# Prologue of an adaLN + MQA + SwiGLU kernel: X tiles first, large weight loads held back, more tile places, evacuation on two engines, new scheduler estimates

## Chip, cores and metric

One core of one Trainium2 chip. Times are device microseconds (us) of that core. A comparison uses runs of the two kernels taken in the same rounds on one chip. The experiments ran on three chips, so kernels of different sessions are compared through their ratios to the kernel before, whose medians in the sessions (1311.0 to 1311.7 us) are close enough for totals to be set side by side to about 1 us. The kernel before takes 1310.71 us (median of 3 runs, 1310.08 to 1313.36).

## The reference, cut to what matters

```python
x: (1, 2048, 1024) bf16;  H = 32 query heads of 32, one key/value head;  F = 3584
mod = silu(c) @ w_mod                     # six vectors of 1024: sa, ca, ga, sb, cb, gb
h = layernorm(x) * (1 + ca) + sa
x = x + ga * attention(h; wq, wk, wv, wo) # softmax over all 2048 keys, no mask
h = layernorm(x) * (1 + cb) + sb
x = x + gb * ((silu(h @ w1) * (h @ w3)) @ w2)
```

Keys and values of all 2048 rows are needed before the first block of queries can be finished. That makes the prologue (load X, normalise, transpose, project to K and V) a gate for the attention.

## The kernel before

The kernel describes all work as a graph of nodes. A list scheduler then fixes, at build time, the order of instructions on every engine. It uses an estimate of each node's duration. The program fixes each engine's order, so **an estimate does not change how long an instruction takes; it changes what stands before it.**

```python
# estimates
def act_t(n):                 return n / 1200.0 + 0.115      # ScalarE: 0.968 us for 1024 elements
def dve_t(n, rate=1):         return n / rate / 960.0 + 0.08
MM = 512 / 2400.0 + 0.0026                                   # one 512-column matmul: 0.2159 us
# in schedule(): a DMA
st = max(dma_free, s + 1.2); dma_free = st + n.nbytes / 230e3
# in schedule(): TensorE takes scores ("S") as soon as they can start, then PV and
# denominators ("V", "D"), and fills what is left with other matmuls
def key(c):
    s, n = c
    if n.cls == "S":            r = 0
    elif n.cls is not None:     r = 1 if att or t - n.est > 1.0 else 4
    else:                       r = 3
    return (r, n.prio, n.seq)
```

The prologue (cut):

```python
xload(0, 4)                                        # X tiles 0-3, 256 KB each
for k in range(NC): dma(... WM01[:, k, :] ...)     # 8 x 512 KB: shift and scale weights
dma(... WKV ...); dma(... WQ[:, :, 0:P] ...)       # wk, wv, first piece of wq
xload(4, 4)
dma(... WQ[:, :, P:D] ...)                         # 1792 KB
dma(... WO ...)                                    # 2048 KB
# [...]
for tb in range(NTB):                              # four blocks of 512 rows
    for i in range(4): ln_stats(tb * 4 + i)        # VectorE
    ln_scale(tb * 4, 4)                            # GpSimd
    for i in range(4): ln_norm(tb * 4 + i, i)      # VectorE, into XN[0..3]
    if tb + 2 < NTB: xload(tb * 4 + 8, 4)          # X has 8 places
    ln_transpose(..., ("act", "dve") if tb == 0 else ("dve",))   # TensorE, evacuated by ScalarE / VectorE
    kv(tb)
    if tb == 0: qproj(0, 0)
```

The attention of one block of 512 queries has 8 groups of 4 heads and 16 tiles of keys, so 128 score steps. One step is four score matmuls (side by side in the array), two exponentials of 128x1024 on ScalarE, and some time later the product with V (PV). In all there are 512 score steps and 1024 exponentials. The kernel uses eight PSUM banks; the scores take six of them and everything else shares two. While ScalarE works on a step, TensorE runs "fillers": Q projections, then the output projection and the MLP (W1, W3, W2) of the block before. The last block's MLP has no attention left to hide behind.

The softmax here doesn't subtract the row's maximum and nothing guards it: scores larger than these inputs give would overflow.

## Time and profile before

Three parts of the page: share of busy time, and the slices of the span (one digit is a fortieth, in tenths).

```profile
span 1308.6 us, 21172 instructions
...
PE 1138.8 (87%) x8561; PEld 439.4 (34%) x8689; DVE 958.9 (73%) x1206; ACT 1015.3 (78%) x1142; POOL 17.1 (1%) x35
...
PE   5387896455779999999899999999999999999998
...
ACT  1368988999999999999979999998999998011100
...
PEclk8688996666889999999999999999999999999999
...
L656 ACT ACTIVATE UREG<-SP 128x1024 bf16<-128x1024 f32 x1024 | 968.5, 1067 | 85.5 <-PE SP L646 65.9
```

ScalarE is at 9 tenths for most of the span and at 0 or 1 in the last six slices, where TensorE is at 9 (8 in the last). So there are two regimes: ScalarE sets the pace until its last exponential, TensorE after it. The Trainium skill (Perfetto Trace Analysis, "Optimization Strategy") says that kernels can have regimes with different most-contended engines, and that interleaving them can pay; this trace has two such regimes.

The stretches of the next view are: to the 16th exponential, to 129, to the end of the Q projections, scores almost without fillers, attention with the MLPs, tail. Columns: stretch, length, then busy time and number of instructions of PE, PEld, DVE, ACT, POOL, then the granted TensorE clock, DMA share, GB/s.

```profile
0.00:49.50 49.50, 23.71 (x315) 14.58 (x321) 29.58 (x60) 19.36 (x22) 5.93 (x17) 0.84 0.84 290
49.50:129.00 79.50, 55.12 (x571) 24.53 (x571) 62.42 (x98) 47.52 (x51) 2.94 (x6) 0.78 0.32 100
129.00:213.00 84.00, 76.30 (x642) 27.74 (x648) 68.31 (x80) 78.10 (x84) 0.00 (x0) 0.95 0.09 26
213.00:373.00 160.00, 91.27 (x756) 24.34 (x763) 108.81 (x119) 146.86 (x158) 1.01 (x2) 0.68 0.09 19
373.00:1107.70 734.70, 698.59 (x5318) 258.03 (x5395) 613.07 (x729) 706.75 (x800) 5.76 (x8) 1.00 0.35 90
1107.70:1308.60 200.90, 193.85 (x980) 90.15 (x997) 76.71 (x122) 16.74 (x29) 1.47 (x3) 0.99 0.53 127
```

The last exponential ends at 1107.7 us; after it come 200.9 us of almost unbroken TensorE work. In the stretch 213 to 373 TensorE has no fillers until 335 us (then some of WO), and its clock was granted at 0.68. The Trainium skill (TensorE: Matmul & The Clock Gate, "What's actually happening") says that an idle array runs at half rate; a mean of 0.68 in the stretch with the most idle time of TensorE (68.7 of 160 us) agrees with the direction. The share of idle time alone does not give the clock, though: in the first stretch TensorE is idle for 52% of the time, and the clock was 0.84.

The timeline of ScalarE from 26 to 90 us shows the prologue's cost. Columns: start, length, engine, line, operation; in brackets the idle time before it and what ended it.

```profile
29.18 1.94 ACT L656 ACTIVATE UREG<-SP 128x1024 bf16<-128x1024 f32 x2 [8.00 <-PE SP L646]
35.36 3.77 ACT L656 ACTIVATE UREG<-SP 128x1024 bf16<-128x1024 f32 x4 [4.25 <-PE SP L646]
39.96 9.27 ACT L656 ACTIVATE UREG<-SP 128x1024 bf16<-128x1024 f32 x10 [0.82 <-PE SP L646]
73.86 7.44 ACT L656 ACTIVATE UREG<-SP 128x1024 bf16<-128x1024 f32 x8 [24.64 <-PE SP L646]
```

Sixteen exponentials run (keys of rows 0 to 1023), then nothing for 24.64 us. The timeline of the DMA queue (SPq) from 10 to 80 us says why:

```profile
17.00 2.89 SPq L409 DMA_DIRECT2D X<-in_A_x_dram  x4
19.94 0.43 SPq L422 DMA_DIRECT2D WREG<-in_A_wq_dram  x1
20.41 0.88 SPq L424 DMA_DIRECT2D WO<-in_A_wo_dram  x1
21.33 10.25 SPq L581 DMA_DIRECT2D WREG<-in_w_mod_dram  x3
31.70 39.35 SPq L409 DMA_DIRECT2D X<-in_A_x_dram  x16
```

And the timeline of VectorE from 44 to 62 us:

```profile
49.33 1.23 DVE L702 TENSOR_TENSOR UREG<-UREG 128x2048 bf16<-128x2048 bf16 x1 [0.60 <-ACT UREG L656]
50.47 1.28 DVE L461 BATCH_NORM_STATS2 ST<-X 128x6 f32<-128x512 bf16 x2
53.03 0.69 DVE L682 COPY ASB<-PB 128x512 f32<-128x512 f32 x1 [1.27 <-PE PB L670]
```

X tiles 8 to 15 are issued from 31.70 us on, behind wq (L422), wo (L424) and three modulation weights (L581); the last eight of the x16 are later loads, from 60.57 us. VectorE starts their statistics (L461) at 50.47 us. In its fixed order they stand behind the sums of the exponentials (L702), for which it waited 0.60 us just before. The queue is not the only cause: the first of these tiles had landed at 40.99 us, so the last 9.5 us before its statistics are due to VectorE's order, fixed beforehand by the scheduler.

To compare whole runs, I use the **delay** of ScalarE. A packed exponential is counted as 0.9246 us (12.94 us for 14 of them), an interleaved tanh as about 0.48 us. Delay at the n-th exponential = its start − (n − 1) × 0.9246 − 0.48 × tanh so far. Before: 29.2 us at the first, 59.1 at the 17th, 67.4 at the 69th, 74.9 at the 151st, 120.5 at the last.

The Trainium skill (ScalarE: Activation LUTs, "What ACT_TABLE_LOAD costs") gives 186 ns + 0.833 ns per element for an activation with immediate scale and bias and an overlap of about 93 ns; for 1024 elements that is 1039 − 93 = 946 ns, an estimate from the page; the trace has 904 from start to start.

### The profile page before, as it was taken

To read this page: it belongs to the slowest core of one execution; us is meant where nothing else is said; L and a number is where in the kernel's file an instruction comes from. 1 tells how busy PE (TensorE), PEld (TensorE's weight loads), DVE (VectorE), ACT (ScalarE), POOL (GpSimd) and SP (SyncE) were. 2 spreads that over 40 slices of the span, in tenths; PEclk is the share of its full clock that TensorE was granted. 3 is DMA by queue.
4 is the path that set the end of the run, shared out by engine and by line. 5 is a ranking of instruction groups with operands and counts; after the bars stand their busy time and mean duration, and the time that the engine had idled before them with its cause. 6 is when DMAs were issued, how large, how long until landed. Compare 5 with 4: busy or idle time off the path is not lost.

```text
span 1308.6 us, 21172 instructions
## 1 busy us (share of the span) xinstructions
PE 1138.8 (87%) x8561; PEld 439.4 (34%) x8689; DVE 958.9 (73%) x1206; ACT 1015.3 (78%) x1142; POOL 17.1 (1%) x35
## 2 busy tenths in 40 slices
PE   5387896455779999999899999999999999999998
PEld 3133331111223333333333333333333333444443
DVE  5768786666798888778978887789888887643421
ACT  1368988999999999999979999998999998011100
POOL 1000000000000000000000000000000000000000
PEclk8688996666889999999999999999999999999999
DMA  9415104000003333342423333441533334375545
GB/s 313 151 41 178 33 1 110 12 1 1 1 1 97 98 97 97 94 85 57 120 78 94 95 94 94 93 77 29 157 97 98 97 97 85 77 175 147 160 83 118
DMA packets 253504, 118.93 MB, mean 91 GB/s; under 512 B 121312, under 2 KB 245216, under 8 KB 253408
## 3 DMA queue, kind: packets, MB, share of 16 engines
q1 hardware_dynamic: 253408, 117.59, 33.9%
q8 instruction: 68, 1.11, 0.4%
q14 instruction: 28, 0.23, 0.1%
HBM read 113.38 MB, written 4.19 MB: 90 GB/s over the span
## 4 chain that ended last, share of the span: by engine, by line
PE 58%; ACT 25%; DVE 9%; issue 6%; DMA 1%; POOL 1%; SPq 0%; DVEq 0%; ACTq 0%
ACT UREG L656 24%; PE PB L765 13%; PE PB L794 10%; PE PB L670 8%; PE SP L646 7%; PE SP L765 6%; PE SP L794 4%; PE PB L546 3%; PE PB L738 2%; ACT HREG L774 2%; DVE UREG L697 2%; DVE ST L461 1%; DVE UREG L702 1%; PE PB L712 1%; PE SP L738 1%
## 5 line engine op out<-in xcount | busy, mean ns | idle before, releaser
L656 ACT ACTIVATE UREG<-SP 128x1024 bf16<-128x1024 f32 x1024 | 968.5, 1067 | 85.5 <-PE SP L646 65.9
L765 PE MATMUL PB<-QT,WREG 128*128 128x512 bf16 x1397 | 343.3, 381 | 9.1 <-issue 6.4
L702 DVE TENSOR_TENSOR UREG<-UREG 128x2048 bf16<-128x2048 bf16 x256 | 310.5, 1213 | 38.4 <-ACT UREG L656 35.9
L646 PE MATMUL SP<-QT,KT 32*128 32x512 bf16 x2048 | 215.4, 411 | 100.0 <-ACT UREG L656 93.9
L697 DVE TENSOR_TENSOR UREG<-UREG 128x2048 bf16<-128x2048 bf16 x128 | 155.8, 1217 | 70.0 <-ACT UREG L656 69.9
L765 PEld LDWEIGHTS PB<-QT,WREG 128*128 128x128 bf16 x1456 | 125.7, 98 | 176.2 <-issue 52.3
L646 PEld LDWEIGHTS SP<-QT,KT 32*128 32x128 bf16 x2048 | 52.0, 92 | 313.4 <-ACT UREG L656 287.0
L794 PE MATMUL PB<-HREG,WREG 128*128 128x512 bf16 x612 | 153.3, 380 | 4.0 <-issue 2.5
L670 PE MATMUL PB<-UREG,V 128*32 128x512 bf16 x2016 | 142.9, 419 | 6.2 <-ACT UREG L656 5.8
L721 DVE RECIPROCAL DSB<-DSB 128x128 f32<-128x128 f32 x128 | 115.5, 928 | 0.1
L774 ACT ACTIVATE HREG<-SP 128x512 bf16<-128x512 f32 x28 | 16.7, 597 | 126.8 <-PE SP L765 123.9
L781 DVE TENSOR_TENSOR HREG<-HREG,PB 128x512 bf16<-128x512 bf16 x98 | 66.3, 676 | 19.6 <-PE PB L765 18.6
L794 PEld LDWEIGHTS PB<-HREG,WREG 128*128 128x128 bf16 x644 | 55.3, 98 | 73.5 <-issue 22.9
L765 PE MATMUL SP<-QT,WREG 128*128 128x512 bf16 x330 | 74.5, 379 | 0.3
L670 PEld LDWEIGHTS PB<-UREG,V 128*32 128x32 bf16 x2016 | 48.0, 101 | 78.9 <-issue 32.4
L776 DVE SCALAR_TENSOR_TENSOR HREG<-HREG,PB 128x512 bf16<-128x512 bf16 x84 | 57.5, 685 | 13.0 <-ACT HREG L774 9.9
L546 PE MATMUL PB<-HREG,WREG 128*128 128x512 bf16 x243 | 62.2, 389 | 1.7 <-DVE QT L549 0.8
L774 ACT ACTIVATE HREG<-PB 128x512 bf16<-128x512 f32 x84 | 56.5, 672 | 6.9 <-PE PB L765 6.8
L794 PE MATMUL SP<-HREG,WREG 128*128 128x512 bf16 x245 | 56.0, 379 | 0.4
L738 PE MATMUL PB<-WO,QT 128*128 128x512 bf16 x193 | 51.0, 389 | 2.9 <-DVE X L741 1.2
L776 DVE SCALAR_TENSOR_TENSOR HREG<-HREG,SP 128x512 bf16<-128x512 bf16 x28 | 19.3, 688 | 43.4 <-ACT HREG L774 43.4
L765 PEld LDWEIGHTS SP<-QT,WREG 128*128 128x128 bf16 x336 | 32.8, 98 | 39.4
(81 smaller groups left out, 547.9 us busy)
## 6 DMA issues: line engine op xcount, KB each, us to landing
WREG<-in_B_w_dram SPq DMA_DIRECT2D x112, 512.0 KB, 3.9
WREG<-in_B_w_dram SPq DMA_DIRECT2D x32, 896.0 KB, 5.9
X<-in_A_x_dram SPq DMA_DIRECT2D x32, 256.0 KB, 3.6
WREG<-in_w_mod_dram SPq DMA_DIRECT2D x16, 512.0 KB, 5.0
UREG<-in_w_mod_dram SPq DMA_DIRECT2D x8, 512.0 KB, 7.9
out_dram<-X SPq DMA_DIRECT2D x16, 256.0 KB, 2.6
WO<-in_A_wo_dram SPq DMA_DIRECT2D x1, 2048.0 KB, 14.6
WREG<-in_A_wq_dram SPq DMA_DIRECT2D x1, 1792.0 KB, 9.6
```

The source lines that it names most:

```text
L546: g = mm_group(NC, lambda e, b, c: e.matmul(b, WQ[:, c, f * P:(f + 1) * P], HT[:, c, sl], start=c == 0, stop=c == NC - 1), lambda c: [("WQ ...
L646: r = e.matmul(SP[:, bufs[gg // 2], gg % 2, j * qn:(j + 1) * qn], KT[32 * gg:32 * gg + 32, kt * P:(kt + 1) * P], QT[32 * gg:32 * gg + 32, ...
L656: G.add("act", lambda e, u=u, h=h, b=bufs[h]: e.activation(U[:, u, 2 * h:2 * h + 2, 0:npk * qn], SP[:, b, :, 0:npk * qn], ACT.Exp, scale=S ...
L670: r = e.matmul(PB[g.bank][32 * gg:32 * gg + 32, 0:qn], V[:, kt, :], U[:, pu, gg, j * qn:(j + 1) * qn], start=w0 + n == 0 and j == 0, stop= ...
L697: G.add("dve", lambda e, tr=tr, u=u, fu=first_u: e.tensor_tensor(TR[:, tr, :, 0:npk * qn], U[:, fu, :, 0:npk * qn], U[:, u, :, 0:npk * qn] ...
L702: G.add("dve", lambda e, tr=tr, u=u: e.tensor_tensor(TR[:, tr, :, 0:npk * qn], TR[:, tr, :, 0:npk * qn], U[:, u, :, 0:npk * qn], ALU.add), ...
L721: G.add("dve", lambda e, h=h: e.reciprocal(DSB[:, h * 128:(h + 1) * 128], DSB[:, h * 128:(h + 1) * 128]), reads=["DSB"], writes=[("DSBr", ...
L738: g = mm_group(NC, lambda e, b, f, t=t, h=h: e.matmul(b, QT[:, f, t * P:(t + 1) * P], WO[:, f, h * 512:(h + 1) * 512], start=f == 0, stop= ...
L765: return e.matmul(b[:, o:o + qn], w13[w][:, sl, c, sub * P:(sub + 1) * P], QT[:, c, q0:q0 + qn], start=c == 0, stop=c == NC - 1)
L774: G.add("act", lambda e, g=g1: e.activation(TS[:, 0:qn], PB[g.bank][:, 0:qn], ACT.Tanh, scale=0.5), writes=["TS"] + alias("TS"), groups=[( ...
L776: G.add("dve", lambda e, g=g1: e.scalar_tensor_tensor(TT[:, 0:qn], TS[:, 0:qn], 1.0, PB[g.bank][:, 0:qn], ALU.add, ALU.mult), reads=["TS"] ...
L794: return e.matmul(b[:, j * qn:(j + 1) * qn], W2S[:, (d0 + j) % 2, fc, :], HHT[:, fc, 0:qn], start=fc == 0, stop=fc == NF - 1)
```

## The change

The intent: get K and V of all rows sooner, so that the exponentials run on without a hole; and give the scheduler better durations. The diff, cut to its core:

```diff
-    xload(0, 4)
+    xload(0, 8)
     (modulation weights, wk, wv, first piece of wq)
-    xload(4, 4)
-    dma(... WQ[:, :, P:D] ..., "wq1", ...)
-    dma(... WO ..., "wo", ...)
 # block loop
+        q0 = 4 if tb == 1 else 0                 # block 1 is normalised into four new places
-            ln_norm(tb * 4 + i, i)
+            ln_norm(tb * 4 + i, q0 + i)
-            xload(tb * 4 + 8, 4)
+            xl = xload(tb * 4 + 8, 4)
-        ln_transpose(4, 0, ..., ("act", "dve") if tb == 0 else ("dve",))
+        ln_transpose(4, q0, ..., ("act", "dve") if tb < 2 else ("dve",))
+    dma(... WQ[:, :, P:D] ..., "wq1", ..., after=xl)     # order only: after the last X loads
+    wo_load = dma(... WO ..., "wo", ..., after=xl)
     (modulation weights of the later parts)  +  after=[wo_load]
 # estimates
-    return n / 1200.0 + 0.115          # act_t: exponential 0.968 us
+    return n / 1200.0 + 0.057          #        exponential 0.910 us
-    dur=act_t(w) + 0.19                # ScalarE evacuation in ln_transpose
+    dur=act_t(w)
-    dma_free = st + n.nbytes / 230e3
+    dma_free = st + n.nbytes / 300e3
-    ln_norm dur=0.5,  reciprocal dur=dve_t(1024) (1.147),  X add dur=dve_t(n * P)
+    ln_norm dur=0.42, reciprocal dur=0.87,                 X add dur=dve_t(n * P, 2)
```

The four new places lie in a buffer's tail that is idle in the prologue. The change's name speaks of the prologue; the last part moves instructions in the whole kernel.

More of the change, by code (lines that the diff above doesn't have):

```diff
@@ L16 @@
                  "start", "vis", "pos", "ndeps", "users", "need_inc", "cnt", "dsem", "dval", "nbytes", "est", "cls",
-                 "sbanks")
+                 "sbanks", "after")
 class Group:
@@ L39, in add @@
     def add(self, eng, fn, reads=(), writes=(), dur=0.1, lat=0.1, prio=5, mode=None, cls=None,
-            acq=None, groups=(), seq=None, dkey=None, nbytes=0, sbanks=()):
+            acq=None, groups=(), seq=None, dkey=None, nbytes=0, sbanks=(), after=()):
         n = Node()
@@ L83, in add @@
             d.users.append(n)
+        n.after = [d for d in after if id(d) not in deps]
+        for d in n.after:
+            assert d.eng == eng
+            d.users.append(n)
         n.dsem = n.dval = None
@@ L103, in schedule @@
         for n in self.nodes:
-            n.ndeps = len(n.deps)
+            n.ndeps = len(n.deps) + len(n.after)
             n.est = 0.0
@@ L229, in schedule @@
                 u.ndeps -= 1
-                if not (e == "pe" and u.eng == "pe"):
+                if not (e == "pe" and u.eng == "pe") and n not in u.after:
                     u.est = max(u.est, n.vis + SEM_LAT)
@@ L400, in build, with dma @@
           reads=["IDENT"], writes=["IDENT"], dur=0.4)
-    def dma(fn, key, reads=(), writes=(), nbytes=0, prio=5, seq=None):
-        return G.add("sp", fn, reads=reads, writes=writes, dur=0.06, dkey=key, nbytes=nbytes, prio=prio, seq=seq)
+    def dma(fn, key, reads=(), writes=(), nbytes=0, after=()):
+        return G.add("sp", fn, reads=reads, writes=writes, dur=0.06, dkey=key, nbytes=nbytes, after=after)
     dma(lambda e: e.dma_start(CROW[:], c_in.rearrange("o (k p) -> (o k) p", p=P)), "c", writes=["CROW"], nbytes=2048)
     def xload(t0, n):
+        r = []
         for t in range(t0, t0 + n):
-            dma(lambda e, t=t: e.dma_start(X[:, t % NXS, :], x2[t * P:(t + 1) * P, :]),
-                ("x", t % NXS), writes=[("X", t % NXS)], nbytes=P * D * 2)
-    xload(0, 4)
+            r.append(dma(lambda e, t=t: e.dma_start(X[:, t % NXS, :], x2[t * P:(t + 1) * P, :]),
+                         ("x", t % NXS), writes=[("X", t % NXS)], nbytes=P * D * 2))
+        return r
+    xload(0, 8)
     for k in range(NC):
@@ L420, in build @@
         writes=[("WQ", 0)] + WQK, nbytes=P * D * 2)
-    xload(4, 4)
-    dma(lambda e: e.dma_start(WQ[:, :, P:D], wq_in[:, P:D].rearrange("(c p) f -> p c f", p=P)), "wq1",
-        writes=[("WQ", 1)], nbytes=7 * P * D * 2)
-    dma(lambda e: e.dma_start(WO[:], wo_in.rearrange("(c p) f -> p c f", p=P)), "wo", writes=["WO"], nbytes=D * D * 2)
     G.add("act", lambda e: e.activation(CT[:], CROW[:], ACT.Tanh, scale=0.5), reads=["CROW"], writes=["CT"], dur=0.25)
@@ L474, in ln_scale, with xnt, xnk @@
               reads=rk + ks, writes=[("NM", t0 + i) for i in range(n)], dur=0.3)
+    def xnt(q):
+        return XN[:, q, :] if q < 4 else UREG[:, (NU + NTR - 2) * 2048 + (q - 4) * D:][:, 0:D]
+    def xnk(q):
+        return [] if q < 4 else [("UR", NU + NTR - 2 + (q - 4) // 2)]
     def ln_norm(t, q):
         s = t % NXS
-        G.add("dve", lambda e: e.tensor_scalar(XN[:, q, :], X[:, s, :], RS[:, t:t + 1], NM[:, t:t + 1],
+        G.add("dve", lambda e: e.tensor_scalar(xnt(q), X[:, s, :], RS[:, t:t + 1], NM[:, t:t + 1],
                                                ALU.mult, ALU.subtract),
-              reads=[("X", s), ("RS", t), ("NM", t)], writes=[("XN", q)], dur=0.5, prio=2)
+              reads=[("X", s), ("RS", t), ("NM", t)], writes=[("XN", q)] + xnk(q), dur=0.42, prio=2)
     def ln_transpose(nt, q0, dst, dkeys, fs, fm, engs, prio=5):
@@ L492, in tr @@
                         r = e.transpose(PBH[g.bank][:, h * w + i * P:h * w + (i + 1) * P],
-                                        XN[:, q0 + i, c * P:(c + 1) * P], IDENT[:])
+                                        xnt(q0 + i)[:, c * P:(c + 1) * P], IDENT[:])
                     return r
-                G.add("pe", tr, reads=[("XN", q0 + i), "IDENT"], dur=ncb * 0.065, lat=0.2,
+                G.add("pe", tr, reads=[("XN", q0 + i), "IDENT"] + xnk(q0 + i), dur=ncb * 0.065, lat=0.2,
                       acq=g if i == 0 else None, groups=[(g, "w")], mode="F", prio=prio)
@@ L504, in ln_transpose @@
                         reads=[("MODC", fs), ("MODC", fm)], writes=dkeys(c), groups=[(g, "r")],
-                        dur=act_t(w) + 0.19, prio=2)
+                        dur=act_t(w), prio=2)
                 else:
@@ L558, in build @@
         ln_scale(tb * 4, 4)
+        q0 = 4 if tb == 1 else 0
         for i in range(4):
-            ln_norm(tb * 4 + i, i)
+            ln_norm(tb * 4 + i, q0 + i)
         if tb + 2 < NTB:
-            xload(tb * 4 + 8, 4)
-        ln_transpose(4, 0, lambda c, tb=tb: HT[:, c, tb * 512:(tb + 1) * 512],
-                     lambda c, tb=tb: [("HT", c, tb)], 0, 1, ("act", "dve") if tb == 0 else ("dve",))
+            xl = xload(tb * 4 + 8, 4)
+        ln_transpose(4, q0, lambda c, tb=tb: HT[:, c, tb * 512:(tb + 1) * 512],
+                     lambda c, tb=tb: [("HT", c, tb)], 0, 1, ("act", "dve") if tb < 2 else ("dve",))
         kv(tb)
@@ L567, in build @@
             qproj(0, 0)
+    dma(lambda e: e.dma_start(WQ[:, :, P:D], wq_in[:, P:D].rearrange("(c p) f -> p c f", p=P)), "wq1",
+        writes=[("WQ", 1)], nbytes=7 * P * D * 2, after=xl)
+    wo_load = dma(lambda e: e.dma_start(WO[:], wo_in.rearrange("(c p) f -> p c f", p=P)), "wo", writes=["WO"],
+                  nbytes=D * D * 2, after=xl)
     for f in range(1, NC):
@@ L582, in build @@
                 WMS[:, sl], wmod_in[kb * 512:(kb + 1) * 512, 2 * D + h * 512:2 * D + (h + 1) * 512]
-                .rearrange("(c p) f -> p c f", p=P)), ("wms", sl), writes=wms(sl), nbytes=P * 2048 * 2)
+                .rearrange("(c p) f -> p c f", p=P)), ("wms", sl), writes=wms(sl), nbytes=P * 2048 * 2,
+                after=[wo_load])
             def mm(e, kb=kb, sl=sl, g=g):
@@ L721, in attention @@
                 G.add("dve", lambda e, h=h: e.reciprocal(DSB[:, h * 128:(h + 1) * 128], DSB[:, h * 128:(h + 1) * 128]),
-                      reads=["DSB"], writes=[("DSBr", h), "DSB%d" % h], dur=dve_t(1024), prio=4)
+                      reads=["DSB"], writes=[("DSBr", h), "DSB%d" % h], dur=0.87, prio=4)
             G.add("dve", lambda e, f=f: e.tensor_tensor(QT[:, f, q0:q0 + qn], ASB[:, 0:qn], DSB[:, 0:qn], ALU.mult),
@@ L826, in post @@
                         reads=[("X", s0 + i) for i in range(n)], writes=[("X", s0 + i) for i in range(n)],
-                        groups=[(g, "r")], dur=dve_t(n * P), prio=1)
+                        groups=[(g, "r")], dur=dve_t(n * P, 2), prio=1)
             G.chain = 2
```

## The prediction

> **What bounds the kernel now.** The waits of ScalarE show where its 1024 attention exponentials (L656) stand still. Packed, one takes 0.925 us (12.94 us for 14 in the timeline), so 1024 need 947 us, with 28 tanh per MLP at about 0.48 us. The first exponential starts at 29.2 us; there is one hole of 24.6 us (49.2 to 73.9), where keys of rows 1024 to 2047 are missing: their X tiles are issued behind three queued weight loads (X at 31.7 us) and VectorE's statistics for them start only at 50.5 us. Counting delay as time minus packed work, it is 29 us at the first exponential, 59 at the 17th, 67 at 128 us, 75 at 213 us, 88 at 373 us, 118 at the last (1107.7 us). Then a TensorE-only tail: about 200 us, matmuls every 0.216 us, no gaps. The Trainium skill (TensorE: Matmul & The Clock Gate, "Wait — 56ns, not 53.3ns?") gives 215.7 ns for 512 columns warm; the tail agrees. So: ScalarE to 1108 us, TensorE after.
>
> **What the change does.**
> 1. Eight X tiles first: 1 MB ahead of the modulation weights, which land about 2.6 us later (estimate from 380 GB/s of the DMA row); shift and scale at about 20.8 instead of 18.1 us.
> 2. X tiles 8 to 15 go before the large loads and land near 24 us. Tiles 4 to 7 are normalised early into the four new places; block 1 is transposed before the first scores, its evacuation shared with ScalarE (four times 0.7 us). The first exponentials slip to about 34 to 38 us, with one further wait, but after about 41 us they should run on: the 17th near 56 us instead of 73.9. Gain about 17 us; 3 to 4 more around the modulation loads.
> 3. The scheduler's durations change everything downstream. It now thinks an exponential takes 0.910 us (was 0.968), so between scores TensorE gets six filler matmuls, not seven. The instruction orders show what that defers: after the last scores, before has 875 filler matmuls left (363 W2, 64 WO, 448 W1/W3), after 981. 106 more at 0.216 us plus 16 transposes make the tail about 24 us longer.
> 4. Between scores: long clumps at the MLP hand-over go (31 matmuls + PV, which cost 8.5 us at 661 to 671 us), W2 steps lose their 0.035 us stretch, together about 14 us; but in the W1/W3 stretches the new order has seven matmuls directly before 32 PV (3.3 us between two scores) about eleven times, where before none was over 2.2 us: about 13 us back.
>
> **Sum.** Last exponential about 20 to 28 us earlier, tail 24 us longer: near zero. The first part is on the critical path, but its gain moves into the tail. I predict 1306 us, 1294 to 1317 in 8 of 10; faster by over 2% 0.07, within 2% 0.91, slower 0.02.
>
> **What would show it.** The 24.6 us hole gone, its remains under 8 us; first exponential later than 29.2 us; last exponential near 1084 us; tail from there about 222 us instead of 200; waits of 1 to 2 us of ScalarE behind TensorE's PV (L685) once per 16 score steps in the W1/W3 stretches; exponentials packed at 0.925 us in the W2 stretches.
>
> **What would make it wrong.** If the 3.3 us clumps are hidden (tanh work covers part), the last exponential falls to 1070 us and the kernel gains over 1%. If X tiles 8 to 15 land late, or block 1's evacuation holds the score banks, the prologue gains under 10 us and the kernel is slower.

## The result, and the profile after

The changed kernel takes 1313.58 us (median of 4, 1313.21 to 1315.52), the kernel before 1311.88 us (median of 4). Ratios in this document are the mean time of one kernel's fast runs over that of the other's in the same rounds, so they are not quite the ratio of the medians. Here it is 1.0017, 95% interval 0.9998 to 1.0035: the same, while a gain of about 5 us had been predicted.

The same parts of the page, of the changed kernel:

```profile
span 1311.2 us, 21296 instructions
...
PE 1168.0 (89%) x8689; PEld 436.1 (33%) x8689; DVE 953.9 (73%) x1202; ACT 1009.4 (77%) x1146; POOL 18.2 (1%) x35
...
PE   5788984547799999999999999999999999999998
...
ACT  1798899898999999999999999999999991011100
...
L671 ACT ACTIVATE UREG<-SP 128x1024 bf16<-128x1024 f32 x1024 | 964.4, 1144 | 67.0 <-PE PB L685 40.6
```

TensorE's busy share reads 87% before and 89% after, but hardly any of that is a difference of the kernels: the trace before holds only 8561 matmul records beside 8689 weight loads, the trace after 8689 of each, and 128 records at 0.216 us are about 27.6 of the 29.2 us of difference. The Trainium skill (Trainium Kernel Development and Optimization, "Performance Expectations") calls matmul busy time a bad metric of the distance to the limit; here the missing records are one more reason not to read it.

The timeline of ScalarE, changed kernel, from its start on (L510 is the evacuation, L671 the exponentials):

```profile
21.20 2.79 ACT L510 ACTIVATE HREG<-SP,MODC 128x512 bf16<-128x512 bf16 x4 [18.77 <-DVE MODC L455]
31.41 1.45 ACT L510 ACTIVATE HREG<-PB,MODC 128x512 bf16<-128x512 bf16 x2 [7.43 <-PE PB L501]
32.76 1.45 ACT L510 ACTIVATE HREG<-SP,MODC 128x512 bf16<-128x512 bf16 x2
37.90 1.94 ACT L671 ACTIVATE UREG<-SP 128x1024 bf16<-128x1024 f32 x2 [3.70 <-PE SP L661]
43.12 20.28 ACT L671 ACTIVATE UREG<-SP 128x1024 bf16<-128x1024 f32 x22 [3.29 <-PE SP L661]
64.05 25.79 ACT L671 ACTIVATE UREG<-SP 128x1024 bf16<-128x1024 f32 x28 [0.65 <-PE SP L661]
```

The hole is gone: from 43.12 us the exponentials run on. The first comes later (37.90 instead of 29.18), and the 17th at 56.0 instead of 73.9 us. The DMA queue of the changed kernel:

```profile
19.90 3.92 SPq L414 DMA_DIRECT2D X<-in_A_x_dram  x8
23.87 0.67 SPq L578 DMA_DIRECT2D WREG<-in_A_wq_dram  x1
24.60 0.78 SPq L580 DMA_DIRECT2D WO<-in_A_wo_dram  x1
25.41 10.90 SPq L595 DMA_DIRECT2D WREG<-in_w_mod_dram  x3
```

X tiles 8 to 15 are issued at 19.90 us, ahead of wq (L578) and wo (L580).

The stretches of the changed kernel, cut at the same work (attention with the MLPs, tail):

```profile
350.00:1087.00 737.00, 703.89 (x5293) 246.43 (x5285) 606.81 (x722) 700.44 (x800) 7.19 (x9) 0.99 0.33 85
1087.00:1311.00 224.00, 217.23 (x1109) 100.26 (x1107) 80.46 (x130) 16.72 (x28) 1.47 (x3) 1.00 0.54 128
```

| | before | changed | difference |
|---|---|---|---|
| delay at the 17th exponential | 59.1 | 41.2 | −17.9 |
| delay at the 69th | 67.4 | 45.6 | −21.8 |
| delay at the 151st | 74.9 | 52.5 | −22.4 |
| delay at the last | 120.5 | 99.3 | −21.2 |
| growth of the delay, 151st to last | 45.6 | 46.8 | +1.2 |
| end of the last exponential | 1107.7 | 1086.1 | −21.6 |
| from there to the end | 200.9 | 225.1 | +24.2 |

The prologue gained 22 us, nearly all of it reached the last exponential (21.6), and then the tail took 24 us back.

What the tail is made of can be counted in the order of TensorE's instructions, which the build fixes: after the last scores the kernel before has 875 filler matmuls left, the changed kernel 981. The weight loads in the two traces give the same counts.

Where ScalarE waits, from the 151st exponential on (engine, line, what it waited for: us in total, times, longest). Before:

```profile
ACT UREG L656 <- PE SP L646: 20.6, 37, 2.2
ACT UREG L656 <- PE PB L670: 11.6, 6, 3.7
ACT HREG L774 <- PE PB L765: 6.8, 4, 3.2
```

Changed:

```profile
ACT UREG L671 <- PE PB L685: 33.4, 20, 2.8
ACT UREG L671 <- PE SP L661: 14.7, 17, 1.7
ACT HREG L789 <- PE PB L780: 0.2, 1, 0.2
```

The waits moved. Behind scores and behind the MLP (L765, L780) they fell by 5.9 and 6.6 us; behind PV (L670, L685) they rose by 21.8 us. One of the new ones, in the timeline of TensorE, changed kernel:

```profile
481.88 0.39 PE L661 MATMUL SP<-QT,KT 32*128 32x512 bf16 x4
482.21 1.69 PE L780 MATMUL PB<-QT,WREG 128*128 128x512 bf16 x7
484.65 1.91 PE L685 MATMUL PB<-UREG,V 128*32 128x512 bf16 x32 [0.76 <-DVE HREG L791]
486.49 0.40 PE L661 MATMUL SP<-QT,KT 32*128 32x512 bf16 x4
```

The same moment in the timeline of ScalarE, changed kernel:

```profile
477.78 4.96 ACT L671 ACTIVATE UREG<-SP 128x1024 bf16<-128x1024 f32 x5
482.37 0.86 ACT L789 ACTIVATE HREG<-PB 128x512 bf16<-128x512 f32 x1
485.31 4.69 ACT L671 ACTIVATE UREG<-SP 128x1024 bf16<-128x1024 f32 x5 [2.08 <-PE PB L685]
```

Scores at 481.88, seven W1/W3 matmuls, then PV, and the next scores only at 486.49. ScalarE does not lack scores here: those of 481.88 are done by 482.27, and it starts again at 485.31, before the next ones. It waits for a place to write. Each score step writes its exponentials into one of ten buffers in turn (NU = 10 in the kernel), and one PV reads the buffers of eight steps. The exponential at 485.31 belongs to step 218 (counted from 0); its buffer is that of step 208, the first that this PV reads, and it starts just after the first eight of PV's 32 matmuls. All 20 waits behind PV in the view above are at such a step (the third of eight), with its scores done. PV itself is late because of the seven matmuls before it, and then waits 0.76 us for L791, the VectorE instruction that empties a W1/W3 result: with only two PSUM banks outside the scores, PV waits until one is emptied. The gap on ScalarE is 2.08 us, and it returns every 34.5 us (450.85, 485.31, 519.78) for as long as the pattern lasts. The Trainium skill (Perfetto Trace Analysis, "Optimization Strategy") says that consistent bubbles can mean that SBUF or PSUM has run out for the next tile; this trace fits, with the ten exponential buffers in SBUF and the two PSUM banks. Both are read from the trace; no run had more of either.

### The profile page after: what moved, and what is told of

It reads as the page before. It is cut to its first block, busy times and chain, and to the rows that moved or that the text cites. A ratio compares the mean times of both kernels' runs of the same rounds, so it can differ in the third digit from the quotient of the medians.

```text
span 1311.2 us, 21296 instructions
## 1 busy us (share of the span) xinstructions
PE 1168.0 (89%) x8689; PEld 436.1 (33%) x8689; DVE 953.9 (73%) x1202; ACT 1009.4 (77%) x1146; POOL 18.2 (1%) x35
## 4 chain that ended last, share of the span: by engine, by line
PE 48%; ACT 34%; DVE 10%; issue 5%; DMA 2%; SPq 1%; POOL 0%; POOLq 0%; DVEq 0%; ACTq 0%
ACT UREG L671 32%; PE PB L780 13%; PE PB L809 7%; PE SP L661 6%; PE SP L780 6%; PE SP L809 5%; PE PB L685 4%; DVE UREG L712 2%; PE PB L753 2%; DVE UREG L717 2%; PE PB L555 2%; ACT HREG L789 2%; PE PB L727 2%; DVE DSB L736 1%; DMA UREG<-in_w_mod_dram 1%
## 5 line engine op out<-in xcount | busy, mean ns | idle before, releaser
L671 ACT ACTIVATE UREG<-SP 128x1024 bf16<-128x1024 f32 x1024 | 964.4, 1144 | 67.0 <-PE PB L685 40.6
L780 PE MATMUL PB<-QT,WREG 128*128 128x512 bf16 x1448 | 354.7, 380 | 2.4 <-DVE QT L516 0.9
L780 PEld LDWEIGHTS PB<-QT,WREG 128*128 128x128 bf16 x1448 | 122.7, 98 | 178.4 <-issue 63.0
L685 PE MATMUL PB<-UREG,V 128*32 128x512 bf16 x2016 | 140.7, 412 | 13.1 <-DVE HREG L791 7.6
L809 PE MATMUL PB<-HREG,WREG 128*128 128x512 bf16 x560 | 143.8, 385 | 0.6 <-DVE DSB L733 0.6
L780 PE MATMUL SP<-QT,WREG 128*128 128x512 bf16 x344 | 77.0, 379 | 0.0
L809 PE MATMUL SP<-HREG,WREG 128*128 128x512 bf16 x336 | 75.8, 379 | 1.0 <-DMA WREG<-in_B_w_dram 1.0
L685 PEld LDWEIGHTS PB<-UREG,V 128*32 128x32 bf16 x2016 | 47.1, 100 | 87.2 <-issue 29.3
L809 PEld LDWEIGHTS PB<-HREG,WREG 128*128 128x128 bf16 x560 | 48.4, 98 | 65.3 <-issue 23.8
L555 PE MATMUL PB<-HREG,WREG 128*128 128x512 bf16 x256 | 66.7, 394 | 1.2 <-DVE QT L558 0.9
L791 DVE SCALAR_TENSOR_TENSOR HREG<-HREG,PB 128x512 bf16<-128x512 bf16 x84 | 57.5, 685 | 10.9 <-ACT HREG L789 4.4
L789 ACT ACTIVATE HREG<-PB 128x512 bf16<-128x512 f32 x84 | 64.6, 769 | 0.2 <-PE PB L780 0.2
L753 PE MATMUL PB<-WO,QT 128*128 128x512 bf16 x216 | 56.4, 390 | 0.9 <-DVE QT L738 0.7
L791 DVE SCALAR_TENSOR_TENSOR HREG<-HREG,SP 128x512 bf16<-128x512 bf16 x28 | 19.3, 688 | 43.7 <-ACT HREG L789 43.7
L780 PEld LDWEIGHTS SP<-QT,WREG 128*128 128x128 bf16 x344 | 33.5, 98 | 40.5 <-issue 0.4
```

What stands on the lines that cost most here:

```text
L555: g = mm_group(NC, lambda e, b, c: e.matmul(b, WQ[:, c, f * P:(f + 1) * P], HT[:, c, sl], start=c == 0, stop=c == NC - 1), lambda c: [("WQ ...
L671: G.add("act", lambda e, u=u, h=h, b=bufs[h]: e.activation(U[:, u, 2 * h:2 * h + 2, 0:npk * qn], SP[:, b, :, 0:npk * qn], ACT.Exp, scale=S ...
L685: r = e.matmul(PB[g.bank][32 * gg:32 * gg + 32, 0:qn], V[:, kt, :], U[:, pu, gg, j * qn:(j + 1) * qn], start=w0 + n == 0 and j == 0, stop= ...
L753: g = mm_group(NC, lambda e, b, f, t=t, h=h: e.matmul(b, QT[:, f, t * P:(t + 1) * P], WO[:, f, h * 512:(h + 1) * 512], start=f == 0, stop= ...
L780: return e.matmul(b[:, o:o + qn], w13[w][:, sl, c, sub * P:(sub + 1) * P], QT[:, c, q0:q0 + qn], start=c == 0, stop=c == NC - 1)
L789: G.add("act", lambda e, g=g1: e.activation(TS[:, 0:qn], PB[g.bank][:, 0:qn], ACT.Tanh, scale=0.5), writes=["TS"] + alias("TS"), groups=[( ...
```

## The experiments

Theory A: the change is two changes with opposite signs. The load order gains about 22 us; the new estimates lengthen the tail and put clumps before PV, which costs about as much. The rivals are named in the expectations. All timed runs are 3 rounds, all results correct. "Left" is the number of fillers after the last scores.

| kernel | left | us (median) | ratio to before, 95% interval | delay at 69th | growth 151st to last | last exponential ends | tail (profiled run) |
|---|---|---|---|---|---|---|---|
| before | 875 | 1310 to 1312 | | 67.4 | 45.6 | 1107.7 | 200.9 |
| changed | 981 | 1313.58 | 1.0017 (0.9998, 1.0035) | 45.6 | 46.8 | 1086.1 | 225.1 |
| a_old_estimates | 875 | 1293.18 | 0.9857 (0.9825, 0.9890) | 45.5 | 47.4 | 1088.9 | 200.9 |
| b_new_estimates | 981 | 1327.66 | 1.0127 (1.0107, 1.0146) | 60.1 | 46.7 | 1100.4 | 224.6 |
| a_old_act_estimate | 903 | 1280.16 | 0.9760 (0.9743, 0.9776) | 45.1 | 32.9 | 1070.4 | 208.4 |
| x4_after_weights | 903 | 1292.91 | 0.9860 (0.9840, 0.9881) | 56.5 | 32.2 | 1081.2 | 208.2 |
| no_extra_places | 903 | 1280.53 | 0.9761 (0.9742, 0.9780) | 45.2 | 32.4 | 1070.3 | 209.1 |
| one_engine_evac | 903 | 1281.94 | 0.9778 (0.9761, 0.9796) | 46.4 | 32.4 | 1071.3 | 208.1 |
| loads_only | 903 | 1280.94 | 0.9770 (0.9751, 0.9788) | 45.8 | 32.2 | 1071.1 | 208.0 |
| weights_not_held | 903 | 1296.64 | 0.9887 (0.9868, 0.9905) | 60.6 | 31.9 | 1085.3 | 208.1 |
| act_as_measured | 1052 | 1307.31 | 0.9967 (0.9949, 0.9984) | 45.3 | 26.8 | 1061.9 | 241.6 |
| act_085 | 1037 | 1301.50 | 0.9924 (0.9909, 0.9939) | 46.8 | 24.0 | 1061.0 | 238.5 |
| act_125 | 872 | 1292.71 | 0.9860 (0.9835, 0.9884) | 46.9 | 48.8 | 1088.2 | 200.9 |
| act_140 | 864 | 1293.09 | 0.9865 (0.9845, 0.9884) | 46.4 | 51.9 | 1090.4 | 199.2 |

### The two halves of the change, apart

`a_old_estimates`: the changed kernel with the six estimates of before.

```diff
-    return n / 1200.0 + 0.057
+    return n / 1200.0 + 0.115
     (and evacuation + 0.19, DMA 230e3, ln_norm 0.5, reciprocal dve_t(1024), X add dve_t(n * P))
```

> The changed kernel with all six of the scheduler's duration estimates put back (ScalarE, transposed-block evacuation, DMA rate, normalise, reciprocal, X add); load order, four places and two-engine evacuation stay. Its instruction order has 875 filler matmuls after the last scores, as before. Theory A (the prologue gains about 22 us and the new estimates cost about 27): about 1290 us, 1284 to 1296; delay of ScalarE about 46 us at the 34th score step, last exponential near 1086 us, tail about 201 us. Rival B (a gain of the prologue is lost in the later blocks whatever the estimates, since TensorE bounds them): about 1312 us.

Measured 1293.18 us, 1.4% faster than before; last exponential at 1088.9, tail 200.9 us. Rival B is out: the prologue's gain is real and reaches the end if the tail keeps its length.

`b_new_estimates`: the kernel before with the six estimates of the change (the diff above the other way round, nothing else).

> The kernel before with only the six new duration estimates; old load order, no new places. Its order has 981 filler matmuls after the last scores and 17 clumps over 2.4 us between two scores, as the changed kernel. Theory A: about 1338 us, 1330 to 1346 (24.6 us hole still there, tail about 224 us). Rival B: about 1312 us.

Measured 1327.66 us, 1.3% slower. The tail is as expected, 224.6 us. The total is 10 us below the expectation, because the estimates also rearrange the prologue (the statistics of X tile 8 start at 44.26 instead of 50.47 us): the delay at the 69th exponential is 60.1, not 67.4. So the new estimates gain 7 us there and lose 24 in the tail. From the medians, the edits of the prologue alone (loads, places, evacuation) are worth −18.5 us (1293.18 against 1311.69) and the estimates alone +16.0 (1327.66 against 1311.69); their sum, −2.5, is within 5 us of the +1.7 of both together. The traces show that the halves are apart: by the tile names of its weight loads, TensorE's order in `a_old_estimates` is that of the kernel before from the 1510th of 8689 on, and in `b_new_estimates` that of the changed kernel from the 597th on.

### Which estimate does the harm

`a_old_act_estimate`: the changed kernel with only ScalarE's estimate put back.

```diff
-    return n / 1200.0 + 0.057
+    return n / 1200.0 + 0.115
-    dur=act_t(w), prio=2
+    dur=act_t(w) + 0.19, prio=2
```

> The changed kernel with only the ScalarE estimate put back (exponential 0.968 us instead of 0.910, evacuation +0.19). Order: 903 filler matmuls left after the last scores, one clump over 2.4 us, sum of excess between scores 23 us (before 35, changed 47). Theory A: about 1284 us, 1278 to 1292, tail about 207 us. Rival C (the other new estimates, of reciprocal and X add, do the harm): about 1310 us.

Measured 1280.16 us, 2.4% faster than before, and the fastest kernel. Tail 208.4 us. Its waits of ScalarE from 191 us on:

```profile
ACT UREG L671 <- PE SP L661: 23.3, 43, 1.7
ACT UREG L671 <- PE PB L685: 1.6, 2, 0.9
```

Behind PV it waits 1.6 us, where the changed kernel waits 33.4. Rival C is out as far as this pair goes: the other new estimates may stay. Against `a_old_estimates`, run in the same rounds, the four of them together even gain 13.0 us (1293.18 to 1280.16).

### Is it the truth of the estimate?

`act_as_measured`, `act_085`, `act_125` and `act_140` change one constant in the changed kernel (its evacuation estimate stays without the 0.19, so they differ from `a_old_act_estimate` in that too, and no run separates the two):

```diff
-    return n / 1200.0 + 0.057
+    return n / 1200.0 + 0.072      # or 0.085, 0.125, 0.14
```

> The changed kernel with the ScalarE constant 0.072 instead of 0.057, so that the scheduler's exponential takes 0.925 us, which is what the trace shows. Order: 1052 fillers left after the last scores (changed 981), sum of excess between scores 36 us (changed 47). Theory A (the time follows the fillers left, at 0.216 us each, plus the excess, not the truth of the estimate): tail about 240 us, total 1318 us, 1310 to 1326. Rival F (a truer estimate gives a faster kernel): below 1305 us.

> The changed kernel with the ScalarE constant 0.085. Order: 1037 left, 4 clumps over 2.4 us instead of 17, excess 25 us instead of 47. Separates clumps from tail: theory A: tail about 237 us, 12 more than the changed kernel, and last exponential about 21 us earlier, so 1304 us, 1296 to 1312. If the clumps cost nothing: about 1325 us.

> The changed kernel with the ScalarE constant 0.125 (exponential 0.978 us). Order: 872 left, excess 28 us, against 903 and 23 in a_old_act_estimate. Theory A: 1278 us, 1273 to 1286.

> The changed kernel with the ScalarE constant 0.14 (exponential 0.993 us). Order: 864 left, excess 30.5 us. Theory A: 1279 us, 1273 to 1290: more fillers between scores now stretch the steps as much as they shorten the tail.

The constant 0.072 makes the scheduler's exponential 0.925 us, the mean of a packed run of 14, which was taken for the true one. The kernel takes 1307.31 us. Rival F is out, and more clearly than it was meant: from start to start the trace has 0.904 us, so the truest of these estimates is the changed kernel's own 0.910, and 0.910 and 0.925 (1313.58 and 1307.31 us) are both slower than 0.968 (1280.16), which is 0.064 us too long. The expectation was 11 us too high, though: the tail is right (241.6 for "about 240"), but the last exponential came 24 us earlier than in the changed kernel, not 11.

`act_085` came out at 1301.50 us for an expected 1304. Its last exponential ends 25.1 us before the changed kernel's, with 4 clumps instead of 17: with fewer clumps ScalarE does stand still less (growth 24.0 against 46.8), but fewer fillers get done and the tail is 238.5 us.

`act_125` and `act_140` missed: 1292.71 and 1293.09 for an expected 1278 and 1279. Their tails are as counted (200.9 and 199.2). The growth of the delay was misjudged: 48.8 and 51.9 us where about 38 and 40 had been expected from `a_old_act_estimate` (32.9 plus the extra excess). Part of the excess lies where no threshold finds it: counting, from the 151st exponential to the last, the time between two starts on ScalarE that exceeds 0.904 us after an exponential and 0.477 after a tanh, `a_old_act_estimate` loses 31.7 us before instructions with a separate wait (over 0.15 us) and 19.4 in spacings without one, `act_125` 38.5 and 28.6, `act_140` 42.9 and 27.3. So the number of fillers left gives the tail reliably, and a sum of excess over a threshold between scores does not give the delay.

Across all versions the tail follows the count: 864 left took 199.2 us, 1052 took 241.6, which is 0.226 us for each filler with its share of transposes.

### Which part of the prologue pays

These five stand on `a_old_act_estimate`. All have the same number of fillers left, and in the first three TensorE's order in the trace is unchanged, so their totals can be compared directly.

`no_extra_places`:

```diff
-        q0 = 4 if tb == 1 else 0
+        q0 = 0
```

> As a_old_act_estimate, but without the four extra places: block 1 is normalised into the same four tiles as block 0. TensorE order unchanged (903 left after the last scores). Theory A: the places buy nothing, since in the changed kernel's trace block 0 is transposed by 16.8 us and block 1 is normalised only from 17.7 us, and block 2 (37.6 us) after block 1's transposes (32.7 us): within 2 us of a_old_act_estimate (1280). Rival E (the places are part of the gain): at least 6 us slower.

`one_engine_evac`:

```diff
-        ("act", "dve") if tb < 2 else ("dve",)
+        ("act", "dve") if tb == 0 else ("dve",)
```

> As a_old_act_estimate, but block 1 is evacuated by VectorE alone. TensorE order unchanged. Theory A: VectorE gets four evacuations of 0.48 us more ahead of block 2's normalising, ScalarE four of 0.7 us less, so 0 to 4 us slower than a_old_act_estimate (1280 to 1284). Rival E: at least 6 us slower.

`loads_only`: both edits together.

> As a_old_act_estimate, with neither the extra places nor the two-engine evacuation: of the prologue only the load order is left. Theory A: 1280 to 1285 us, that is nearly the whole prologue gain. Rival E: 1290 us or more.

Measured 1280.53, 1281.94 and 1280.94 us against 1280.16. Places and two-engine evacuation buy nothing that these runs resolve (their intervals overlap that of `a_old_act_estimate`). Rival E is out. With ScalarE's old estimate, two of the five items in the title are not needed.

`weights_not_held`: eight X tiles first, but wq and wo ahead of X tiles 8 to 15 and nothing held.

```diff
+    dma(... WQ[:, :, P:D] ..., "wq1", ...)      # right after the first piece of wq
+    dma(... WO ..., "wo", ...)
-    (both after the block loop, after=xl)
-    (later modulation weights)  after=[wo_load]
```

> As a_old_act_estimate with eight X tiles first, but the two large weight loads go ahead of X tiles 8 to 15 again and nothing is held. 903 left as well. Theory A: the hole in the exponentials comes back (10 to 20 us) after the 16th exponential; delay at the 69th exponential 56 to 66 us instead of 45; total 1290 to 1300 us. Rival D (what pays is the eight tiles first): within 4 us of a_old_act_estimate.

Measured 1296.64 us. The hole is back, shorter:

```profile
38.99 12.94 ACT L670 ACTIVATE UREG<-SP 128x1024 bf16<-128x1024 f32 x14 [1.56 <-PE SP L660]
69.00 7.44 ACT L670 ACTIVATE UREG<-SP 128x1024 bf16<-128x1024 f32 x8 [17.08 <-PE SP L660]
```

`x4_after_weights`: loads held, but X tiles 4 to 7 after the modulation weights.

```diff
-    xload(0, 8)
+    xload(0, 4)
     (modulation weights, wk, wv, first piece of wq)
+    xload(4, 4)
```

> As a_old_act_estimate, but X tiles 4 to 7 are issued after the modulation weights as in the kernel before; the large weight loads stay held behind X tiles 8 to 15. Theory A: what matters is that the large loads no longer stand before tiles 8 to 15; first exponential back to about 29 to 30 us, no hole over 8 us, delay at the 34th score step within 4 us of a_old_act_estimate, total within 5 us of it. Rival D (the eight tiles first are what pays): at least 10 us slower than a_old_act_estimate.

Measured 1292.91 us, 12.8 us slower than `a_old_act_estimate`. Here theory A missed and rival D's number held: the first exponential comes at 30.4 us, as expected, but the delay at the 69th is 56.5, not 45.1. So both pieces of the load order are needed: without the hold the kernel loses 16.5 us, without the early tiles 12.8. Both of these runs also have another instruction order of TensorE in the prologue (up to weight load 608 without the hold and 1533 without the early tiles), since the scheduler reacts to the loads; what part of their loss is the DMA and what part the order was not separated.

## Why the prediction was right or wrong

**Bounds: right.** ScalarE to its last exponential, TensorE after. 0.216 us per matmul of 512 columns held in the tails of all 14 traces (start to start). The 0.925 us for an exponential was misread (0.904), with no effect on the difference of the kernels.

**Prologue (steps 1 and 2): right.** Shift and scale at 20.9 us (predicted 20.8). First exponential at 37.9 (34 to 38). One further wait, 3.29 us. The 17th at 56.0 (56). Gain 17.9 us at the 17th (17) and 3.9 more by the 69th (3 to 4). Of its means, the four places and the shared evacuation turned out to add nothing that the runs resolve.

**The tail (step 3): right.** Predicted about 24 us longer, measured 24.2. The 106 fillers are in the traces; of transposes there are 8 more after the last scores, not 16.

**Clumps (step 4): both terms too small, their balance nearly right.** "About 13 us back" was predicted for the clumps before PV; the waits behind PV rose by 21.8 us. "Together about 14 us" was predicted for what goes away: behind scores and MLP 12.5 us went, and since the growth of the delay changed by only +1.2 us, another 8.1 us (21.8 − 12.5 − 1.2) must have gone out of steps that show no separate wait. Counted by start spacings, as for `act_125` above, those steps lost 19.0 us before and 6.8 after, and those with a wait 44.9 and 58.2; the difference, +1.1, agrees. That two misjudged terms nearly cancelled is luck. What the clumps hold up was not in the prediction: ScalarE waits for exponential buffers, not for scores. The clumps were not hidden: where a wait of 1 to 2 us was named, it was often 2.1.

**The sum: this is the step that failed.** "Last exponential about 20 to 28 us earlier, tail 24 us longer: near zero. … I predict 1306 us." The terms in the text are 17 + 3 to 4 + (14 − 13), which is 21 to 22 us. The upper half of "20 to 28" had no term behind it. Measured: 21.6 us earlier, 24.2 us longer, so +2.6 us in the profiled runs. The number 1306, about 5 us faster, did not follow from the terms. It is the sum of two figures under "What would show it", 1084 for the last exponential and 222 for the tail. But 1084 is 23.7 us earlier, more than the terms give, and 222 is only 21 us longer than the 200.9 before, less than step 3 gives. The trace has 1086.1 + 225.1 = 1311.2, and the device time is another 2.2 us longer than the trace's span (1313.43 in that run), which the sum left out. The terms themselves, added up, gave 24 − 21.5 = +2.5 us, about 1314, which is what came. With two large terms of opposite sign, the difference has to be written down as the sum says.

**What stays open.** That ScalarE waits for one of ten exponential buffers until a late PV has read it, and that PV waits for a PSUM bank held by a W1/W3 result, was read from the trace and not tested alone: no run had more buffers, or PV in smaller pieces. The separate effects of the new reciprocal, X-add, DMA and normalise estimates were not tested, nor ScalarE's constant apart from the evacuation's 0.19. Why the count of fillers left drops from 1037 to 903 between act_085 and a_old_act_estimate was not traced through the scheduler.

## What to carry to other kernels

When a build-time scheduler fixes the order, treat a change of its estimates as a change of the whole kernel: compare the instruction orders, count what is left over when the long engine finishes, and test the estimates apart from the edit that they came with. Here one half gave 18.5 us, the other took 16, and putting back ScalarE's estimate turned "no change" into 2.4%. A true duration is not automatically the best input of a greedy scheduler. And in a prologue that is gated by data, first look at what the needed loads are queued behind; here the order of loads, with the instruction order that the scheduler built on it, was the whole gain as far as the runs resolve it, and extra buffers and a second evacuating engine added nothing.

## What the Trainium skill lacked or had wrong

- TensorE: Matmul & The Clock Gate, "Back-to-back issue gap", gives about 131 ns per 512-column matmul as the sustained spacing in streams of weight loads and matmuls, and says that N/2.4 + 2.5 ns (216 ns) over-counts there. In this kernel's tail, weight loads and matmuls alternate and 40 matmuls take 8.64 us (from 1169.28 to the next group at 1177.92 us, before): 216 ns each. The formula was right, the sustained figure was not reached.
- ScalarE: Activation LUTs, "What ACT_TABLE_LOAD costs": its figures give 946 ns for packed activations of 1024 elements, the trace 904 ns from start to start. Small, but over 1024 of them it is 43 us.
- No page says that an order fixed at build time can move work between regimes, or to count the leftover work of one engine at the moment another finishes. Here 106 leftover matmuls were 24 us.
